# Softcap attention with a two-stage MLP mixer: the second channel product by pairs of batches in Strassen's seven block products

## The chip, the cores and the metric

The kernel runs on one core of one Trainium2 chip. The core has five engines with a queue each: TensorE (PE) for matrix products into PSUM, VectorE (DVE) and ScalarE (ACT) for elementwise work, GpSimd (POOL), and SyncE (SP), which here only issues DMAs. The metric is the device time of one execution in microseconds, lower is better. Before the change it is 588.58 us, the median of 3 runs (588.46 to 589.6).

## The reference

Four batches, 12 heads, 448 positions, 64 wide. The attention output is the input x (4 x 448 x 768) of a mixer with a token product and a channel product:

```python
scores = cap * np.tanh(scale * np.matmul(q, k.transpose(0, 1, 3, 2)) / cap)
attn = np.exp(scores - np.max(scores, axis=-1, keepdims=True))
attn = attn / (np.sum(attn, axis=-1, keepdims=True) + 1e-09)
x = np.matmul(attn, v)                       # heads side by side: (4, 448, 768)
h = np.maximum(x.transpose(0, 2, 1) @ w_tok1, 0.0) @ w_tok2
u = x + h.transpose(0, 2, 1)
h2 = np.maximum(u @ w_ch1, 0.0) @ w_ch2      # 768 -> 1536 -> 768
return (u + h2).astype(np.float32)
```

## The kernel before

The program has an attention part, a token part that is worked in between, and a channel part that is PE work from about 261 us on. Only the channel part changes.

Each batch has u as six chunks of 128 channels by 448 positions. The 1536 hidden channels go in 6 groups (`NG`) of 2 x 128 (`GF`). For each group and batch, `ch1` makes the hidden block (2 x 6 chunks x 3 matmuls = 36), and `ch2` multiplies it by the group's second weights and adds to all six chunks of u (6 x 2 x 3 = 36). Each product takes three matmuls because every operand is split into a high and a low part in a fast fp32 format (`TERMS`: high x high, low x high, high x low). PE does `ch1` of the next batch before `ch2` of the last one.

After `ch1`, ACT applies the ReLU into the high part of `g` (line 859) and DVE makes the low part (862). After each chunk of `ch2`, DVE adds PSUM to u (line 891); in the last group the chunk is stored at once (893). The weights arrive as 64-bit floats and are decoded in thirds of 512 columns, six thirds per group: ACT takes the magnitude (233), DVE clips (239, 240) and puts sign and low bits back (246, 247), ACT makes the high part (256), DVE the low part (260). The second weights of the next group go to a second buffer.

PSUM has eight banks: `ps_a` two tiles of two banks, `ps_b` and `ps_c` two tiles of one bank each.

The order on every engine is written out by a planner in the code (`Plan`): an operation becomes a job with a cost, its dependencies and a slack, and when PE's planned time passes, jobs that are ready are put into their engine's queue, the one with the smallest ready time plus slack first. The queues then run strictly in order. When the token part is done, `order.close()` (in `first_group`) ends the written order and the rest of the program runs in the order in which it was issued.

The last batch of the last group lies in one arm of a branch on the size of `cap`; the other arm is a general version that these inputs don't reach.

## Time and profile before

| | |
|---|---|
| median of 3 runs | 588.58 us |
| the profiled execution | 588.43 us |
| its span, first to last instruction | 586.6 us |
| PE busy | 580.8 us (99%), 3102 matmuls |
| DVE busy | 404.4 us (69%) |
| ACT busy | 255.2 us (44%) |
| POOL busy | 9.2 us (2%) |

Busy shares are means over the span; the parts of the program have different limits, so a stretch is read by itself. The chain of waits is followed back from the last instruction: where it runs on one engine without a break, that engine sets the time there. The mean of a matmul (366 ns) is its latency; matmuls overlap, and the step from one to the next is read from the chain. On DVE too an instruction's duration is longer than the step to the next start.

### The profile page before, as it was taken

What the parts mean: (1) busy time and instruction counts of PE and PEld (TensorE: products, weight loads), DVE (VectorE), ACT (ScalarE), POOL (GpSimd) and SP (SyncE); (2) the same over time, 40 slices, a digit from 0 to 9 for tenths busy, and PEclk for the clock granted to TensorE, in tenths of its full rate; (3) what the DMA queues carried; (4) which work ended last, traced back from release to release, by engine and by line L of the source; (5) the groups of instructions that cost most, each with busy time, mean ns of one, the idle gap of its engine ahead of it and who ended that gap; (6) DMA issues with size and microseconds to landing.
All of it is one profiled execution on the core that took longest, in us unless ns stands there. A gap on an engine that the chain in (4) does not pass through costs nothing.

```text
span 586.6 us, 7996 instructions
## 1 busy us (share of the span) xinstructions
PE 580.8 (99%) x3102; PEld 450.0 (77%) x3102; DVE 404.4 (69%) x681; ACT 255.2 (44%) x330; POOL 9.2 (2%) x23
## 2 busy tenths in 40 slices
PE   8999999999999999999999999999999999999997
PEld 2233455544646899999999999999999999999996
DVE  2999999998999997468886568356834653333334
ACT  6999999899897343241431213021302120000000
POOL 0000100001000000000000000000000000000000
PEclk9999999999999999999999999999999999999999
DMA  7554766857431041002433032103210200000234
GB/s 228 178 155 127 236 194 195 244 168 220 147 120 53 21 136 37 1 1 73 143 108 108 1 108 72 37 0 108 72 37 0 73 1 0 1 0 5 93 112 172
DMA packets 26779, 55.50 MB, mean 95 GB/s; under 512 B 7024, under 2 KB 16752, under 8 KB 26736
## 3 DMA queue, kind: packets, MB, share of 16 engines
q1 hardware_dynamic: 24288, 48.37, 26.6%
q0 software_dynamic: 2160, 6.39, 3.9%
...
q10 hardware_dynamic: 288, 0.18, 0.1%
q14 instruction: 18, 0.15, 0.1%
...
## 4 chain that ended last, share of the span: by engine, by line
PE 90%; ACT 6%; DVE 1%; issue 1%; DMA 1%; DVEq 0%; ACTq 0%
PE ps_g L849 30%; PE ps_o L881 30%; PE ps_pv L438 7%; PE ps_qk L360 6%; PE ps_h L596 5%; PE ps_u L619 5%; ACT e L390 3%; ACT e L398 3%; PE ps_t L568 2%; PE ps_s L489 2%; PE ps_pv L441 1%; PE ps_qk L371 1%; PE ps_qk L365 1%; DMA qkraw<-in_qk 1%; DVE acc L477 0%
## 5 line engine op out<-in xcount | busy, mean ns | idle before, releaser
L881 PE MATMUL ps_o<-g,wc 128*128 128x448 f32 x864 | 181.2, 366 | 0.0
L881 PEld LDWEIGHTS ps_o<-g,wc 128*128 128x128 f32 x864 | 162.0, 188 | 14.4
L849 PE MATMUL ps_g<-uhl,wc 128*128 128x448 f32 x648 | 138.1, 367 | 0.0
L849 PEld LDWEIGHTS ps_g<-uhl,wc 128*128 128x128 f32 x648 | 121.0, 188 | 11.1 <-issue 0.7
L891 DVE TENSOR_TENSOR u<-u,ps_o 128x448 f32<-128x448 f32 (+1 forms) x145 | 87.3, 614 | 43.3 <-PE ps_o L881 42.9
L390 ACT ACTIVATE e<-ps_qk,tsc 128x896 f32<-128x896 f32 x84 | 81.8, 1040 | 9.5 <-PE ps_qk L360 4.2
L398 ACT ACTIVATE e<-e,near 128x896 f32<-128x896 f32 x84 | 85.7, 1082 | 0.1
L859 ACT ACTIVATE g<-ps_g 128x896 fp32r<-128x896 f32 x24 | 22.0, 916 | 134.5 <-PE ps_g L849 134.3
L862 DVE SCALAR_TENSOR_TENSOR g<-ps_g,g 128x896 fp32r<-128x896 f32 x24 | 26.1, 1088 | 72.4 <-ACT g L859 72.4
L438 PE MATMUL ps_pv<-e,vn 128*64 128x448 f32 x288 | 60.5, 549 | 0.9 <-ACT e L398 0.9
L256 ACT ACTIVATE wc<-wz 128x512 fp32r<-128x512 f32 x36 | 22.8, 634 | 84.2 <-DVE wz L247 37.6
L849 PE MATMUL ps_g<-last_u,wc 128*128 128x448 f32 x216 | 45.6, 368 | 0.0
L438 PEld LDWEIGHTS ps_pv<-e,vn 128*64 128x64 f32 x288 | 18.0, 136 | 34.7 <-issue 25.0
L849 PEld LDWEIGHTS ps_g<-last_u,wc 128*128 128x128 f32 x216 | 40.5, 188 | 4.1
L233 ACT ACTIVATE wz<-wraw 128x512 f32<-128x512 f32 x36 | 24.2, 672 | 37.2 <-DVE wc L260 16.9
L260 DVE TENSOR_TENSOR wc<-wz,wc 128x512 fp32r<-128x512 f32 x36 | 24.7, 687 | 20.1 <-ACT wc L256 19.6
L596 PE MATMUL ps_h<-wc,last_u 128*128 128x384 f32 x176 | 33.3, 337 | 0.0
L619 PE MATMUL ps_u<-last_u,wc 128*128 128x448 f32 x144 | 32.9, 372 | 0.0
L596 PEld LDWEIGHTS ps_h<-wc,last_u 128*128 128x128 f32 x176 | 30.8, 188 | 1.8 <-issue 1.3
L619 PEld LDWEIGHTS ps_u<-last_u,wc 128*128 128x128 f32 x144 | 26.4, 188 | 6.0 <-issue 1.8
L477 DVE TENSOR_TENSOR acc<-acc,e 64x448 f32<-64x448 f32 x48 | 29.7, 618 | 1.3
L460 DVE TENSOR_TENSOR acc<-e 128x896 f32<-128x896 f32 x24 | 25.9, 1078 | 6.6 <-ACT e L398 6.5
...
## 6 DMA issues: line engine op xcount, KB each, us to landing
...
vn<-in_v SPq DMA_DIRECT2D x24, 224.0 KB, 3.3
rb<-rs SPq DMA_DIRECT2D x48, 112.0 KB, 3.4
out_t<-u SPq DMA_DIRECT2D x23, 224.0 KB, 1.9
...
```

Of the source, the lines that this page charges most:

```text
L360: nc.tensor.matmul(ps[:, j, :S], two[x][r, ks], two[y][r, :S], start=(n == 0), stop=(n == 2))
L390: nc.scalar.activation(e, ps[:, :, :S], AF.Tanh, scale=tsc)
L398: nc.scalar.activation(e, e, AF.Exp, scale=near)
L438: nc.tensor.matmul(o, vn[x % 3][:, j * NF + c], es[b, p, c][:, j], start=first, stop=last)
L460: nc.vector.tensor_tensor(accs[b, q][0][:, i], es[b, p, 0], es[b, p, 1], op=ALU.add)
L477: nc.vector.tensor_tensor(t, t, es[b, p - i, NF][r, i], op=ALU.add)
L596: nc.tensor.matmul(ps[:, :HALF], w, x, start=(n == 0), stop=(n == len(mm) - 1))
L619: nc.tensor.matmul(ps[:, :S], h1[:, hi, t, cs], w2s[:, wi, t, :], start=(n == 0), stop=(n == 3 * NT - 1))
L849: nc.tensor.matmul(ps[:, i, :S], w[:, wi, cc, fs], uhl[b][:, ui, cc, :], start=(n == 0), stop=(n == 3 * NC - 1))
L862: nc.vector.scalar_tensor_tensor(x[:, 1], ps[:, :, :S], 0.0, x[:, 0], op0=ALU.max, op1=ALU.subtract)
L881: nc.tensor.matmul(ps[:, :S], w[:, wi, i, cs], x[:, gi, i, :], start=(n == 0), stop=(n == 3 * GF - 1))
L891: nc.vector.tensor_tensor(u[b][:, cc, r], u[b][:, cc, r], ps[:, r], op=ALU.add)
```

## The change

From group 1 on the second product is done for two batches together. The hidden blocks of the two batches (h0, h1 of the first, h2, h3 of the second) are seen as a 2 x 2 block matrix, the group's second weights as another (two hidden halves by two output halves of 3 chunks). Strassen's scheme in Winograd's form needs seven block products instead of eight; a block product here is 3 chunks x 3 matmuls. Group 0 stays as it was.

- The ReLU now goes to an fp32 buffer `hid` (line 912 of the changed kernel). POOL forms four differences in place: x = h3 - h2, t1 = x - h0, t2 = h3 - t1, t4 = h1 - t2 (line 927). ACT and DVE split the seven left operands into high and low parts (946, 950), in a ring of six.
- The weights need three block sums and one difference: four DVE operations of 128 columns (279 to 282) per third, and high and low parts of seven blocks instead of four (287, 288 on ACT; 296, 297 on DVE). The seven blocks of a third have one buffer, so the next group's can be written only after this group's last product.
- The products are chained in PSUM. Chain a takes p1, p6, p5, p3, one onto the other, in three banks; chain b takes p7 and p4, then p2 anew, in three more. After each product DVE adds the chain's present sum to the half of u that it belongs to: in chain a the first two chunks with one wide add (1011), else chunk by chunk (1071). So PE may add the next product of a chain to a bank only when DVE has read it.
- A pair's second product is issued after both first products of the next pair; the last two pairs follow each other. In the last group the sums of p4, p5, p2 and p3 are stored as they are added.
- The written order (`order`) now lasts to the end of the program.

```diff
+MC = NC // 2
+NW = 4
+NS = 3
+NO = 6
+PRODUCTS = (
+    ("p1", 0, "h0", "a", 0, 0),
+    ("p7", 1, "x", "b", 1, 1),
+    ("p6", 5, "t2", "a", 1, 0),
+    ("p4", 3, "t4", "b", 1, 0),
+    ("p5", 4, "t1", "a", 1, 1),
+    ("p2", 2, "h1", "b", 0, 0),
+    ("p3", 6, "h3", "a", 0, 1),
+)
...
+            if sums is not None:
+                job("dve", 4 * 190, 4 * 190 + 70, blocks, (*key, 3), ("m2",), room("ws"), slack=slack, key=(*key, 5))
+                return
...
+        def blocks():
+            z = bits(held["z"]).rearrange("p (k c) -> p k c", k=NW)
+            s = held["s"] = late["m2"].tile([P, NS, P], F32, tag="ws", name="ws", bufs=2)
+            held["ws"] = rings["ws"].take(1)
+            add, sub = ALU.add, ALU.subtract
+            nc.vector.tensor_tensor(s[:, 0], z[:, 1], z[:, 3], op=add)
+            nc.vector.tensor_tensor(z[:, 1], z[:, 0], z[:, 1], op=sub)
+            nc.vector.tensor_tensor(s[:, 1], s[:, 0], z[:, 0], op=sub)
+            nc.vector.tensor_tensor(s[:, 2], z[:, 2], s[:, 1], op=sub)
+            job("act", 935, 1040, high, (*key, 5), *after, slack=slack, key=(*key, 4))
+
+        def high():
+            z = bits(held["z"]).rearrange("p (k c) -> p k c", k=NW)
+            nc.scalar.activation(sums[0][:, :NW], z, AF.Copy)
+            nc.scalar.activation(sums[0][:, NW:], held["s"], AF.Copy)
+            j = job(SUB, *((930, 1010) if SUB == "dve" else (2400, 2480)), low, (*key, 4), slack=slack, key=key)
+            held["wz"].read(j)
+            held["ws"].read(j)
+
+        def low():
+            z = bits(held["z"]).rearrange("p (k c) -> p k c", k=NW)
+            e = nc.vector if SUB == "dve" else nc.gpsimd
+            e.tensor_tensor(sums[1][:, :NW], z, sums[0][:, :NW], op=ALU.subtract)
+            e.tensor_tensor(sums[1][:, NW:], held["s"], sums[0][:, NW:], op=ALU.subtract)
...
+    wsum = [wset[i][1][:, :2 * (NW + NS) * P].rearrange("p (x k c) -> p x k c", x=2, k=NW + NS) for i in range(2)]
+    wend = [wset[i][1][:, 2 * (NW + NS) * P:3 * (NW + NS) * P].rearrange("p (k c) -> p k c", k=NW + NS) for i in range(2)]
+    wblock = [(wsum[i][:, 0], wsum[i][:, 1]) for i in range(2)] + [tuple(wend)]
...
+        late["o"] = m1.tile([P, NO, 2, S], F32R, name="ops", bufs=1)
+        late["h"] = m1.tile([P, 5, S], F32, name="hid", bufs=1)
...
+    def relu(g, b, ps, hold):
+        h = late["h"]
+        n, j = (g, b // 2), b % 2
+        old = late.get("last")
+        if j == 0:
+            free = [("s", old, k) for k in ("p4", "p2")] if old else []
+        else:
+            free = [("s", old, k) for k in ("p5", "p3")] if old else []
+
+        def take():
+            nc.scalar.activation(h[:, 2 * j:2 * j + 2], ps[:, :, :S], AF.Relu)
+
+        hold.read(job("act", 891, 960, take, plan.pe + DRAIN, *free, slack=-300.0, key=("r", n, j)))
+        if j == 1:
+            operands(n, old)
+            late["last"] = n
...
+    def operands(n, old):
+        h = late["h"]
+        place = {"h0": 0, "h1": 1, "t1": 2, "h3": 3, "x": 4, "t2": 0, "t4": 0}
+
+        def form(key, out, a, b, *deps):
+            e, cost = (nc.gpsimd, (1170, 1250)) if FORM == "gps" else (nc.vector, (536, 620))
+            job(FORM, *cost, lambda: e.tensor_tensor(h[:, out], h[:, a], h[:, b], op=ALU.subtract),
+                *deps, slack=500.0, key=("f", n, key))
+
+        form("x", 4, 3, 2, ("r", n, 1), *([("s", old, "p7")] if old else []))
+        form("t1", 2, 2, 0, ("f", n, "x"), ("r", n, 0))
+        form("t2", 0, 3, 2, ("f", n, "t1"), ("s", n, "p1"))
+        form("t4", 0, 1, 0, ("f", n, "t2"), ("s", n, "p6"))
+        source = {"h0": ("r", n, 0), "h1": ("f", n, "t4"), "h3": ("f", n, "t2")}
+        before = None
+        for k, _, of, *_ in PRODUCTS:
+            deps = [source.get(of, ("f", n, of)), room("o")] + ([("sh", n, before)] if before else [])
+            split(n, k, h[:, place[of]], deps)
+            before = k
+
+    def split(n, k, src, deps):
+        def high():
+            i = len(rings["o"].holds) % NO
+            t = late["o"][:, i]
+            operand[n, k] = t, rings["o"].take(1)
+            nc.scalar.activation(t[:, 0], src, AF.Copy)
+
+        def low():
+            t = operand[n, k][0]
+            nc.vector.tensor_tensor(t[:, 1], src, t[:, 0], op=ALU.subtract)
+
+        job("act", 468, 568, high, *deps, slack=800.0, key=("sh", n, k))
+        job("dve", 536, 620, low, ("sh", n, k), slack=800.0, key=("s", n, k))
...
+        seen = {"a": 0, "b": 0}
+        for k, a, _, chain, i, j in PRODUCTS:
+            await_key(("s", n, k))
+            x, of = operand[n, k]
+            b = 2 * q + j
+            first = k in ("p1", "p7", "p2")
+            done_now = last and k in ("p4", "p5", "p2", "p3")
+            for mc in range(MC):
+                await_key(("wc2", g, mc))
+                if not first or k == "p2":
+                    await_key(("o", n, chain, mc, seen[chain] - 1))
+                ps = banks[chain][mc]
+                for m, (wi, xi) in enumerate(TERMS):
+                    nc.tensor.matmul(
+                        ps[:, :S], wblock[mc][wi][:, a], x[:, xi], start=first and m == 0, stop=m == 2,
+                        skip_group_check=not first,
+                    )
+                plan.spend(3 * 204)
+                wide = chain == "a" and mc < 2 and not done_now
+                if wide and mc == 0:
+                    continue
+                cc = MC * i + mc
+                if wide:
+                    o = job("dve", 1010, 1092, lambda b=b, cc=cc: add_two_out(b, cc - 1, two), plan.pe + DRAIN, slack=URGENT,
+                            key=("o", n, chain, 0, seen[chain]))
+                    done["o", n, chain, 1, seen[chain]] = o
+                    holds_of["a"][0].read(o)
+                else:
+                    o = job("dve", 530, 612, lambda b=b, cc=cc, ps=ps, d=done_now: add_out(b, cc, ps, d), plan.pe + DRAIN,
+                            slack=URGENT, key=("o", n, chain, mc, seen[chain]))
+                    if chain == "b":
+                        holds_of["b"][mc].read(o)
+                    elif mc == 2:
+                        holds_of["a"][1].read(o)
+                    elif mc == 1:
+                        holds_of["a"][0].read(o)
+                fill()
+            of.read(plan.pe)
+            seen[chain] += 1
+
+    def add_two_out(b, cc, ps):
+        nc.vector.tensor_tensor(u[b][:, cc:cc + 2], u[b][:, cc:cc + 2], ps[:, :, :S], op=ALU.add)
...
-                order.close()
...
+            ch1(w[0], b, g, b // 2)
+            if g == 1 and b == 0:
+                ch2(*pend)
+                done["ch2", 0] = plan.pe
             if g == NG - 1 and b == 0:
                 tc.mark_branch_hint_location("big", hint="LikelyTaken", engines=(engines.PE,))
-            ch2(*pend)
-            if pend[1] == B - 1:
-                done["ch2", pend[4]] = plan.pe
-            pend = (w[1], b, gt, g == NG - 1, g)
+            if b % 2:
+                if before is not None:
+                    ch2_pair(before, False)
+                    if before[1] == 1:
+                        done["ch2", before[0]] = plan.pe
+                before = g, b // 2
...
-        gt = ch1(w[0], B - 1, NG - 1)
-        ch2(*pend)
-        ch2(w[1], B - 1, gt, True, NG - 1)
+        ch1(w[0], B - 1, NG - 1, 1)
+        ch2_pair((NG - 1, 0), True)
+        ch2_pair((NG - 1, 1), True)
```

How this moves instructions. On PE, before: the first product of batch 1 in group 2 and then the second product of batch 0 (`ps_g` is the first product's PSUM tile, `ps_o` the second's, `wc1`, `wc2` the weights, `g` the split hidden block).

```order
L849 MATMUL ps_g_3278<-uhl1_2038,wc1_0_79 128x448 x36
L881 MATMUL ps_o_3333<-g_3213,wc2_0_80 128x448 x6
L881 MATMUL ps_o_3345<-g_3213,wc2_0_80 128x448 x6
L881 MATMUL ps_o_3354<-g_3213,wc2_0_80 128x448 x6
L881 MATMUL ps_o_3363<-g_3213,wc2_0_80 128x448 x6
L881 MATMUL ps_o_3373<-g_3213,wc2_0_80 128x448 x6
```

Now, in group 2: the first product of batch 1, and p1 and p7 of the pair of batches 2 and 3 of group 1 (`ps_o2` is the two-bank tile of chain a, `ops` the ring of split operands).

```order
L1024 MATMUL ps_g_3607<-uhl1_2038,wc1_1_81 128x448 x36
L983 MATMUL ps_o2_3665<-ops_2039,wc2_0_80 128x448 x3
L983 MATMUL ps_o2_3665<-ops_2039,wc2_1_82 128x448 x3
L983 MATMUL ps_o_3666<-ops_2039,wc2_0_80 128x448
L983 MATMUL ps_o_3666<-ops_2039,wc2_1_82 128x448
L983 MATMUL ps_o_3666<-ops_2039,wc2_0_80 128x448
L983 MATMUL ps_o_3667<-ops_2039,wc2_0_80 128x448 x3
L983 MATMUL ps_o_3668<-ops_2039,wc2_1_82 128x448 x3
L983 MATMUL ps_o_3669<-ops_2039,wc2_0_80 128x448
L983 MATMUL ps_o_3669<-ops_2039,wc2_1_82 128x448
L983 MATMUL ps_o_3669<-ops_2039,wc2_0_80 128x448
```

Six matmuls in a row on a bank became three, and the same banks come back after 18 matmuls with the next product of their chain.

On DVE, before: the adds of a second product in group 1, batch 0, between weight decoding (`wz`, `wraw`: the third being decoded).

```order
L891 TENSOR_TENSOR u0_75<-u0_75,ps_o_2921 128x448
L247 SCALAR_TENSOR_TENSOR wz_2979<-wraw_2938,wz_2979 128x512
L891 TENSOR_TENSOR u0_75<-u0_75,ps_o_2928 128x448
L239 TENSOR_SCALAR wz_3182<-wz_3182 128x512
L891 TENSOR_TENSOR u0_75<-u0_75,ps_o_2942 128x448
L260 TENSOR_TENSOR wc2_0_80<-wz_2979,wc2_0_80 128x512
L891 TENSOR_TENSOR u0_75<-u0_75,ps_o_2951 128x448
L240 TENSOR_SCALAR wz_3182<-wz_3182 128x512
L246 SCALAR_TENSOR_TENSOR wz_3182<-wraw_3165,wz_3182 128x512
L891 TENSOR_TENSOR u0_75<-u0_75,ps_o_2961 128x448
L247 SCALAR_TENSOR_TENSOR wz_3182<-wraw_3165,wz_3182 128x512
```

Now, at the start of the pair of batches 2 and 3 of group 1: the last piece of weight decoding in front of it, then the adds of p1, p7, p6 and p4 with two splits (`hid` to `ops`) in between.

```order
L267 SCALAR_TENSOR_TENSOR wz_3652<-wraw_3625,wz_3652 128x512
L1011 TENSOR_TENSOR u2_77<-u2_77,ps_o2_3665 128x896
L1071 TENSOR_TENSOR u2_77<-u2_77,ps_o_3666 128x448
L1071 TENSOR_TENSOR u3_78<-u3_78,ps_o_3667 128x448
L1071 TENSOR_TENSOR u3_78<-u3_78,ps_o_3668 128x448
L950 TENSOR_TENSOR ops_2039<-hid_2040,ops_2039 128x448
L1071 TENSOR_TENSOR u3_78<-u3_78,ps_o_3669 128x448
L1011 TENSOR_TENSOR u2_77<-u2_77,ps_o2_3665 128x896
L950 TENSOR_TENSOR ops_2039<-hid_2040,ops_2039 128x448
L1071 TENSOR_TENSOR u2_77<-u2_77,ps_o_3666 128x448
L1071 TENSOR_TENSOR u2_77<-u2_77,ps_o_3667 128x448
```

Weight decoding was spread between the adds; it now stands between the pairs, and the adds have splits between them.

On DVE at the end, before: the adds to batches 2 and 3 in the last group.

```order
L891 TENSOR_TENSOR u2_77<-u2_77,ps_o_4754 128x448
L891 TENSOR_TENSOR u2_77<-u2_77,ps_o_4763 128x448
L891 TENSOR_TENSOR u3_78<-u3_78,ps_o_4772 128x448
L891 TENSOR_TENSOR u3_78<-u3_78,ps_o_4781 128x448
L891 TENSOR_TENSOR u3_78<-u3_78,ps_o_4790 128x448
L891 TENSOR_TENSOR u3_78<-u3_78,ps_o_4799 128x448
L891 TENSOR_TENSOR u3_78<-u3_78,ps_o_4808 128x448
L891 TENSOR_TENSOR u3_78<-u3_78,ps_o_4817 128x224 x2
```

Now, from one of the last two pairs to the other: the end of the pair of batches 0 and 1, and the start of the pair of batches 2 and 3, with the last splits.

```order
L950 TENSOR_TENSOR ops_2039<-hid_2040,ops_2039 128x448
L1071 TENSOR_TENSOR u1_76<-u1_76,ps_o2_4745 128x448 x2
L1071 TENSOR_TENSOR u1_76<-u1_76,ps_o_4746 128x448
L950 TENSOR_TENSOR ops_2039<-hid_2040,ops_2039 128x448 x2
L1011 TENSOR_TENSOR u2_77<-u2_77,ps_o2_4850 128x896
L1071 TENSOR_TENSOR u2_77<-u2_77,ps_o_4858 128x448
L1071 TENSOR_TENSOR u3_78<-u3_78,ps_o_4859 128x448
L950 TENSOR_TENSOR ops_2039<-hid_2040,ops_2039 128x448
L1071 TENSOR_TENSOR u3_78<-u3_78,ps_o_4860 128x448
L950 TENSOR_TENSOR ops_2039<-hid_2040,ops_2039 128x448
L1071 TENSOR_TENSOR u3_78<-u3_78,ps_o_4861 128x448
```

The splits of the last pair stand before and between its adds.

## Rows read from the trace of the kernel before

**Rows 1.** The page's table of busy time: busy us, share of the span, instructions.

```profile
PE 580.8 (99%) x3102; PEld 450.0 (77%) x3102; DVE 404.4 (69%) x681; ACT 255.2 (44%) x330; POOL 9.2 (2%) x23
```

**Rows 2.** The chain that ended last: start us, us, engine, tile, line, instructions.

```profile
261.38 12.27 PE ps_o L881 x60
...
288.44 7.36 PE ps_o L881 x36
295.80 7.36 PE ps_g L849 x36
...
568.52 14.74 PE ps_o L881 x72
```

**Rows 3.** By stage: us; busy us of PE, PEld, DVE, ACT, POOL; clock, DMA share, GB/s.

```profile
347.40:406.36 58.96, 58.96 (x290) 54.06 (x289) 34.44 (x58) 11.18 (x16) 0.00 (x0) 1.00 0.17 54
```

**Rows 4.** Timeline of VectorE, 262 to 265 us: start us, us, instruction.

```profile
263.35 0.62 DVE L720 TENSOR_TENSOR last_u<-u,last_u 128x448 fp32r<-128x448 f32 x1
263.88 0.61 DVE L891 TENSOR_TENSOR u<-u,ps_o 128x448 f32<-128x448 f32 x1
```

**Rows 5.** Timeline of all engines, 566 to 587 us.

```profile
568.36 14.89 PE L881 MATMUL ps_o<-g,wc 128*128 128x448 f32 x72
...
569.86 0.62 DVE L891 TENSOR_TENSOR u<-u,ps_o 128x448 f32<-128x448 f32 x1 [8.11 <-PE ps_o L881]
570.40 1.08 DVE L862 SCALAR_TENSOR_TENSOR g<-ps_g,g 128x896 fp32r<-128x896 f32 x1
...
571.40 0.61 DVE L891 TENSOR_TENSOR u<-u,ps_o 128x448 f32<-128x448 f32 x1
...
583.28 0.68 DVE L891 TENSOR_TENSOR u<-u,ps_o 128x224 f32<-128x224 f32 x2 [0.61 <-PE ps_o L881]
584.00 0.36 ACTq L893 DMA_DIRECT2D out_t<-u  x1
```

**Rows 6.** Timeline of VectorE, 276 to 281 us.

```profile
276.43 0.43 DVE L239 TENSOR_SCALAR wz<-wz 128x512 f32<-128x512 f32 x1 [1.53 <-ACT wz L233]
...
277.36 0.69 DVE L246 SCALAR_TENSOR_TENSOR wz<-wraw,wz 128x512 int32<-128x512 int32 x1
278.08 0.69 DVE L247 SCALAR_TENSOR_TENSOR wz<-wraw,wz 128x512 int32<-128x512 int32 x1
278.69 0.42 DVE L239 TENSOR_SCALAR wz<-wz 128x512 f32<-128x512 f32 x1
...
279.49 0.69 DVE L260 TENSOR_TENSOR wc<-wz,wc 128x512 fp32r<-128x512 f32 x1
280.09 0.68 DVE L246 SCALAR_TENSOR_TENSOR wz<-wraw,wz 128x512 int32<-128x512 int32 x1
```

**Rows 7.** Groups of instructions by form: busy us, mean ns of one, idle before.

```profile
L256 ACT ACTIVATE wc<-wz 128x512 fp32r<-128x512 f32 x36 | 22.8, 634 | 84.2 <-DVE wz L247 37.6 <-PE ps_g L849 36.0 <-PE ps_o L881 10.1
L859 ACT ACTIVATE g<-ps_g 128x896 fp32r<-128x896 f32 x24 | 22.0, 916 | 134.5 <-PE ps_g L849 134.3
...
L579 DVE TENSOR_TENSOR wc<-ps_t,wc 64x128 fp32r<-64x128 f32 x24 | 7.0, 293 | 0.3
```

**Rows 8.** Groups of instructions by form, GpSimd.

```profile
masks.py:199 POOL TENSOR_SCALAR_AFFINE_SELECT ident<-ident 128x128 f32<-128x128 f32 x1 | 0.3, 287 | 0.1
...
L1074 POOL MEMSET const-float32-1.0<- 128x1 f32 x1 | 0.1, 103 | 0.0
```

**Rows 9.** DMA issues: instructions, KB each, median us to landing.

```profile
out_t<-u SPq DMA_DIRECT2D x23, 224.0 KB, 1.9
...
out_t<-u ACTq DMA_DIRECT2D x1, 112.0 KB, 1.7
```

**Rows 10.** Busy time by stage: the fullest DMA of those read; the stores before the end.

```profile
4.00:8.00 4.00, 3.92 (x12) 1.36 (x12) 0.38 (x3) 1.82 (x2) 0.00 (x0) 1.00 0.95 340
...
580.00:584.00 4.00, 3.25 (x16) 2.63 (x15) 2.15 (x5) 0.00 (x0) 0.00 (x0) 1.00 0.54 206
```

More of the change, by code (lines that the diff above doesn't have):

```diff
@@ L53 @@
 PAIRED = (12, 40)
+SUB = "dve"
+END = 2
+FORM = "gps"
+URGENT = -500.0
 class Job:
@@ L208, in room, with like, decode @@
         return rings[n].room
-    def decode(src, n, hi, lo, early, blank, key, slack, since, after):
+    def like(z, to):
+        return z if len(to.shape) == 2 else z.rearrange("p (f m c) -> p f m c", f=GF, m=2)
+    def decode(src, n, hi, lo, early, blank, key, slack, since, after, sums=None):
         held = {}
@@ L280, in group_weights, with second @@
         t2 = t2.rearrange("p (x f c) -> p x f c", x=2, f=GF)
[L281 to L284 removed]
+        st = kw.pop("stagger", 0.0)
+        slack, since = kw.get("slack", 3000.0), kw.get("since", 0.0) + GF * C * st
+        def second(mc):
+            d = t2.rearrange("p x f (m k c) -> p x f m k c", m=2, k=MC)[:, :, :, :, mc]
+            decode(
+                wc2[g][:, mc * DU:(mc + 1) * DU], DU, d[:, 0], d[:, 1], False, None, ("wc2", g, mc),
+                slack, since + mc * DU * st, after[1], wblock[mc] if combine else None,
+            )
+        return (t1, t2), decode_steps(wc1[g], t1, DU, ("wc1", g), after=after[0], stagger=st, **kw) + [
+            lambda mc=mc: second(mc) for mc in range(MC)
+        ]
     in_att, e_att, x_att = ExitStack(), ExitStack(), ExitStack()
@@ L839, in ch1 @@
+    def add_two_out(b, cc, ps):
+        nc.vector.tensor_tensor(u[b][:, cc:cc + 2], u[b][:, cc:cc + 2], ps[:, :, :S], op=ALU.add)
+    def ch1(w, b, g=0, pair=None):
         await_time(rings["a"].room)
         ps = ps_a.tile([P, 2, 512], F32, tag="a", name="ps_g")
-        hold = rings["a"].take(2)
+        hold = rings["a"].take(2 if pair is None else 1)
         for i in range(GF):
@@ L855, in ch1 @@
             open_m1()
-        x = m1.tile([P, 2, GF, S], F32R, tag="g", name="g")
+        if pair is not None:
+            relu(g, b, ps, hold)
+            return None
+        i = 2 * (late.setdefault("n", 0) % 2)
+        late["n"] += 1
+        x = late["o"][:, i:i + 2]
         def high():
@@ L887, in add_out @@
     def add_out(b, cc, ps, last):
-        end = last and b == B - 1 and cc == NC - 1
+        end = last and b == B - 1 and cc == (END if late.get("last") else NC - 1)
         for i, q in enumerate((nc.sync, nc.scalar) if end else (nc.sync,)):
@@ L918, in open_m2 @@
         split_tile(2, pool)
+        late["m2"] = pool
+        done["m2",] = plan.pe
     def first_group(w):
@@ L945, in tile_softcap_mixer @@
     w = w0
+    before, steps_of = None, {}
     for g in range(NG):
+        later = steps_of[g][-MC:] if g > 1 else []
         if g + 1 < NG:
-            nxt, steps = group_weights(
-                g + 1, ([("tok",)], [("tok",)]) if g == 0 else ((), [("ch2", g - 1)]), slack=60000.0
-            )
-            for step in steps:
-                step()
+            nxt, steps_of[g + 1] = group_weights(
+                g + 1, ([("tok",)] if g == 0 else (), [("ch2", g)]), combine=True, slack=60000.0
+            )
+            later = steps_of[g + 1][:len(steps_of[g + 1]) if g == 0 else -MC] + later
+        for step in later:
+            step()
         if g == 0:
@@ L1000, in general @@
     def general():
+        late.pop("last")
         for step in decode_steps(w1, w1s, DU, ("w1",), False, w1s[:LAST, 1, NK - 1]) + decode_steps(w2, w2s, S, ("w2",)):
@@ L1037, in tile_softcap_mixer @@
         general()
+    order.close()
 def kernel(q, k, v, cap, moe_w_tok1, moe_w_tok2, moe_w_ch1, moe_w_ch2):
```

40 lines of the change are left out of this document (26 added, 14 removed).

## The prediction

> **What bounds the kernel now.** I read the busy table first: TensorE (PE) is busy for 580.8 of 586.6 us, VectorE (DVE) for 404.4, GpSimd (POOL) for 9.2 [rows 1]. A busy PE alone proves little, so I took the chain of waits next: from 261.38 us to 583.26 us it runs over PE alone, in pieces of 7.36 us with 36 matmuls each, channel products one and two in turn [rows 2]. That is 204.5 ns from one matmul to the next (14.74 us / 72), without a gap, at a granted clock of 1.00 (the level of 2.4 GHz) in the group looked at [rows 2, 3]. So in this part every matmul that goes takes 0.2045 us off the end, unless PE comes to wait. The third view is the table by stage: in one group of 58.96 us DVE is busy for 34.44 us, ScalarE (ACT) for 11.18, POOL for none [rows 3]. DVE is the engine to watch: nearly all that the change adds goes there.
>
> **What it removes.** Groups 1 to 5 do the second product with 2 x 63 matmuls instead of 4 x 36 = 144. That is 18 less per group, 90 in all: 90 x 0.2045 = 18.4 us. All of them have the same shape as before and stand on the chain. The order of PE up to the first product of group 1 stays as it is.
>
> **What it adds on DVE.** Start-to-start steps are the price in a queue, not durations. 448 columns step 0.535 us (263.35 to 263.88 [rows 4]); 896 columns out of PSUM 1.00 (570.40 to 571.40 [rows 5]); a 512-column two-input operation 0.60 (279.49 to 280.09), a clip pair 0.93 (276.43 to 277.36), a sign-and-low-bits pair 1.33 (277.36 to 278.69) [rows 6]. No row has 128 columns on 128 partitions; 64x128 lasts 293 ns [rows 7], less the 82 ns by which a 0.617 us add overlaps the next it steps 0.21, and 0.33 where it needs the result before it (dependence costs 0.12: 277.36 to 278.08 is 0.72 against 0.60 [rows 6]).
> - Adds of a pair of batches: four products of chain a at 1.00 + 0.535, three of chain b at 3 x 0.535: 10.95 us (12 x 0.535 = 6.4 before).
> - Splits of operands: 7 x 0.535 = 3.75 us (2 x 1.00 before).
> - A third of the second weights: 0.93 + 1.33 + four block sums 1.08 + low parts of 512 and 384 columns 1.07 = 4.41 us, where it was 0.93 + 1.33 + 0.60 = 2.86. A third of the first weights stays at 2.86.
>
> Per group that is 2 x (10.95 + 3.75) + 3 x 4.41 + 3 x 2.86 = 51.2 us. The same sum for before is 24 x 0.535 + 4 x 1.00 + 6 x 2.86 = 34.0 and the trace has 34.44 [rows 3], so the prices hold. PE's group shrinks to 270 x 0.2045 = 55.2 us. DVE goes from 58% of the group to 93%, and its queue is strictly in order: the question is only where PE waits for it. ACT gets 14 splits of at most 0.63 us and three 384-column high parts more: 11.2 + 8.8 + 1.6 = 21.6 of 55.2, so I cost it at nothing beyond the waits below. SP issues the same loads and stores, in thirds as before; the DMA engines are 0.17 busy in such a group [rows 3], so a load that starts later still lands long before its third is decoded.
>
> **Inside a pair.** Let the 63 matmuls start at 0; three matmuls take 0.613, and an add can start 0.27 after the end of its bank (568.36 + 6 x 0.2045 = 569.59, the add starts at 569.86 [rows 5]). The seven products alternate between chain a and chain b, except that p2 starts b anew, so a bank has one product's time, 1.84 us, and the rest of its own, to be read. The wide add of p1 runs 1.50 to 2.51, then in the queue's order: 2.51 to 4.10 three narrow ones, 4.10 a split, 4.64 the last of p7, 5.17 a split, 5.70 to 6.71 the wide add of p6. Chain a is needed again at 3.68 (p6; read by 2.6) and at 7.36 (p5; read by 6.85): 1.0 and 0.5 us to spare. p5's wide add ends at 10.4 and p3 needs it at 11.04: again 0.5. DVE has 13.1 us of work (10.95 + 4 splits) in PE's 12.9, so a delay in front of the pair is not made up within it: what exceeds 0.5 us becomes a PE wait.
>
> What stands in front: from one pair to the next PE takes 72 + 63 matmuls, 27.6 us; DVE does 14.7 of adds and splits and about 10.9 of weights (the 21.8 of a group, halved), 25.6. It also waits in order: for ACT's high part before a low part (0.63 for 512 columns [rows 7], somewhat over 1.1 with the 384) about once per pair, and for POOL's t4 before one split: t4 starts after the fourth split of the pair at 13.1, ends at 14.2, ACT's part at 14.9, where DVE is free at 14.6, so 0.3 to 0.4. So DVE is through at about 27.2 to 28.5 and the first add comes due at 27.6 + 1.5 = 29.1. The cover is 0.6 to 1.9, plus the 0.5 inside.
>
> **POOL's four subtractions per pair.** No row has POOL at two inputs. Below: its one-input select of 128 columns lasts 287 ns and a one-column memset 103 [rows 8], 1.45 ns a column, so 448 take 0.75. Above: twice that per column, 1.4. I take 1.1, the middle, as both ends count the same columns; 40 of them are off the chain at either end. (The Trainium skill, GPSIMD Engine Reference, section 3.1, states about 2.6 cycles per element at 1.2 GHz for two inputs; that is an estimated 0.97 us and the sum would be the same.) The difference x can't start before the ReLU of the pair's second batch (0.916 [rows 7]), which waits for the split of h3 of the pair before it, at 4.7: x, t1, t2 run from about 5.8 to 9.2.
>
> No row shows whether POOL and DVE delay each other, since POOL never computes beside DVE in this trace. If not, nothing is added. If a split must wait for POOL, it is the one at 8.8, at most until t2 ends: 0.4 on average of the phases, which uses up most of the 0.5 to spare. The Trainium skill, SBUF — State Buffer, "Who interferes with whom", says that a DVE instruction with two SBUF inputs and a GpSimd instruction that reads SBUF exclude each other for a whole instruction; here that would hold for splits and weights, not for adds out of PSUM. No row here shows it; by the page the sum would be near rival 1's, without it at the forecast's lower end.
>
> I put 0.3 us of PE wait on each of the first eight pairs: 2.4 us. Ends: 0, and 1.5 (a 1.33 us weight pair just in front of the first add, which then passes 0.5, and a POOL operation in front of a split).
>
> **The last two pairs** follow each other without a first product between them. Chain a's third bank is read by DVE at about 14.6 of the first one; the second wants it at 12.9 + 1.2 = 14.1: 0.6. DVE then carries two splits and three single adds in place of wide ones: another 0.6 at p6 and p5. Together 1.2 (0 to 3; the upper end also for the branch behind which both lie: in the trace DVE stood idle there, 8.11 us before its add [rows 5], and now finds work at once).
>
> **The end.** Before, one 224 KB sum is stored per six matmuls, 1.23 us, and the last lands 1.7 us after its issue at 584.00 [rows 5, 9]. Now twelve are final within PE's last 6.8 us: 2.75 MB. The stores so far ran at 206 GB/s with the DMA engines 0.54 busy, which scales to 381; the fullest window has 340 at 0.95, so 358 [rows 10]. At 365 twelve take 7.5 us. The first is issued some 5.1 us before PE's end, so the last lands 5.1 less, plus 7.5 plus 1.3 (1.9 to land [rows 9] less 0.6 of transfer): 3.7 after PE's end, against 584.00 + 1.7 - 583.26 = 2.45 before: 1.2 us more. Ends: 0, and 5 if stores can't exceed the 206 GB/s seen.
>
> **Sum** against the profiled execution, 588.43 us (span 586.6 and 1.8 around it; 0.15 under the median 588.58): 588.43 - 18.4 + 2.4 + 1.2 + 1.2 = 574.8 us. That PE stands still for under 2 us at a time leaves me no reason in the rows to expect another clock.
>
> **Rivals.**
> 1. *DVE becomes the bound between pairs.* POOL's operations hold up DVE, 2 x 1.1 us in each of eight periods, and the waits for ACT come out at their upper end: 28.5 + 2.2 = 30.7 against 29.1 + 0.5, 1.1 us of wait; with a block sum or a wait mis-sized by 0.4 it is 1.5. 8 x 1.5 = 12, + 1.2 + 1.2: 584.4. For it: 93% and one queue. Against: most DVE work beside t2 and t4 is adds from PSUM.
> 2. *The stores decide the end*, at 206 GB/s: 2.75 MB in 13.3 us; 574.8 + 3.8 = 578.6. For it: no row has more for stores. Against: the engines were half idle then.
> 3. *The chain of operands decides, and the kernel gets slower.* Place: t2 and t4, which need the split before them, POOL, ACT, DVE in turn, while DVE's queue stands at the next split and everything behind it, adds and weights, stands too. If POOL needs 2.4 us, t2 ends at 12.9, the fourth split comes at 13.7 rather than 12.5, t4 at 16.7, and DVE idles 1.8 more before the next split: 28.5 + 3.0 = 31.5 against 29.6, 1.9 per pair. With rival 1's blocking at that length (another 1.5) it is 3.4 x 8 = 27 us: 588.4 - 18.4 + 27 + 2.4 = 599.4. It turns slower from 2.0 us per pair on ((18.4 - 2.4) / 8). Against: 2.4 is 1.7 times my upper end for POOL.
> 4. *The change doesn't do what it says*: a matmul that adds to a bank read in between steps slower than one in a run of six. At 0.02 us a matmul, 630 x 0.02 = 12.6 us: 574.8 + 12.6 = 587.4, no change that can be told. Against: [rows 2] show one step across bank changes.
>
> **How the numbers follow.** Forecast 0.68, from 570 (no wait, end as before: 588.4 - 18.4) to 578.5; rival 1 0.16; rival 2 0.07; rival 3 0.06; rival 4 0.03. A measurement of this kernel tells 0.2%, 1.2 us, from no change. Forecast, rival 2 and nearly all of rival 1 are faster: 0.91. Same 0.03, from the rest of rival 1 and part of rival 4; slower 0.06. The range goes from 570 up to 583.5, into rival 1; 0.12 lies above it and a little below.
>
> **What would show it.** Right: 774 second-product matmuls instead of 864, still about 204.5 ns apart; 40 POOL subtractions near 1.1 us; DVE over 85% busy from group 1 to 4; PE idle in small pieces, at the wide adds (p5, p3) and in the last pair, under 5 us in sum; the last stores landing close behind each other. Wrong: PE waits of over 1 us at the first product of a pair (then the weights are late, rival 1), splits that wait for ACT behind POOL (rival 3), splits whose duration grows beside POOL (blocking), or a step above 210 ns (rival 4).

## The result and the profile after

The changed kernel takes 572.69 us, the median of 4 runs (572.08 to 572.91), against 588.52 us (587.63 to 589.60) for the kernel before, run beside it: a ratio of 0.9729, 95% interval 0.9711 to 0.9747. The forecast was 574.8. The profiled execution took 572.91 us with a span of 571.1; before it was 588.43 and 586.6, so 15.5 us are to be accounted for.

The page's table of busy time, which answers to [rows 1]:

```profile
PE 561.6 (98%) x3012; PEld 432.1 (76%) x3012; DVE 491.7 (86%) x860; ACT 299.0 (52%) x415; POOL 57.5 (10%) x63
```

There are 90 matmuls less, 87 us more of DVE work and 40 instructions more on POOL. The chain that ended last (start us, us, engine, tile, line, instructions) answers to [rows 2]:

```profile
318.09 13.14 PE ps_o L983 x63
331.23 14.72 PE ps_g L1024 x72
345.95 12.88 PE ps_o L983 x63
...
484.17 12.88 PE ps_o L983 x63
```

From 318 to 511.8 us (497.05 + 14.72, the next piece) it is PE alone; behind that the view follows other engines, although PE's own timeline, below, shows no further wait up to 556 us. A pair's second product takes 12.88 us, 63 x 0.2045: a matmul that adds to a bank read in between steps no slower than one in a run of six. Stages of the program (us; busy us of PE, PEld, DVE, ACT, POOL with counts; granted clock, DMA share, GB/s), the first a whole group as in [rows 3], the others a window of the last stores at full rate and what follows PE's last matmul:

```profile
331.23:386.50 55.27, 55.27 (x272) 50.62 (x271) 51.38 (x94) 19.88 (x33) 9.50 (x8) 1.00 0.19 58
...
563.00:565.00 2.00, 2.00 (x12) 1.83 (x11) 2.00 (x5) 0.00 (x0) 0.00 (x0) 1.00 1.05 402
...
566.56:571.10 4.54, 0.00 (x0) 0.00 (x0) 1.18 (x4) 0.00 (x0) 0.00 (x0) 0.99 0.69 256
```

PE's group is 55.27 us (forecast 55.2), DVE's share of it 51.38 (forecast 51.2). PE's timeline has the places at which it waited, in brackets with the releaser:

```profile
318.09 13.14 PE L983 MATMUL ps_o<-ops,wc 128*128 128x448 f32 x63 [0.49 <-ACT hid L912]
...
539.28 16.97 PE L983 MATMUL ps_o<-ops,wc 128*128 128x448 f32 x81
556.62 3.97 PE L983 MATMUL ps_o<-ops,wc 128*128 128x448 f32 x18 [0.37 <-DVE u L1011]
560.81 5.75 PE L983 MATMUL ps_o<-ops,wc 128*128 128x448 f32 x27 [0.22 <-DVE u L1011]
```

One wait of 0.49 us stands in front of the first pair, none at the next seven, two lie in the last two pairs. A duration in this view holds the last matmul's latency, so a delay is read from start to start: the first pair starts 8.09 us after the 36 matmuls in front of it (310.00 to 318.09), the third one 7.43 (366.03 to 373.46), which makes that wait cost 0.65. PE ends at 566.56; from 539.28 that is 27.28 us for 126 matmuls, whose steps make 25.77 and the last one's end 0.16 more, so 1.35 are lost. The span goes on for 4.54 us after PE, before for 3.34. The sum: -18.4 for the matmuls, +0.65, +1.35, +1.2 for the end, and -0.35 because the channel part starts at 261.02 instead of 261.38 us: -15.55, against -15.5 measured. The -0.35 is not the change's work; the runs below differ by more than that in front of the first pair.

VectorE in front of the first pair (start us, us, instruction), and then GpSimd and ScalarE there:

```profile
304.31 1.35 DVE L308 TENSOR_TENSOR wc<-wz,wc 128x512 fp32r<-128x512 f32 x1 [0.22 <-ACT wc L304]
305.59 1.64 DVE L296 TENSOR_TENSOR wc<-wz,wc 128x512 fp32r<-128x512 f32 x1
307.15 1.51 DVE L297 TENSOR_TENSOR wc<-ws,wc 128x384 fp32r<-128x384 f32 x1
...
311.96 1.53 DVE L267 SCALAR_TENSOR_TENSOR wz<-wraw,wz 128x512 int32<-128x512 int32 x1
...
315.81 0.68 DVE L308 TENSOR_TENSOR wc<-wz,wc 128x512 fp32r<-128x512 f32 x1
316.41 0.62 DVE L950 TENSOR_TENSOR ops<-hid,ops 128x448 fp32r<-128x448 f32 x1
```

```profile
303.85 4.40 POOL L927 TENSOR_TENSOR hid<-hid 128x448 f32<-128x448 f32 x3 [146.71 <-ACT hid L912]
...
317.12 0.92 ACT L912 ACTIVATE hid<-ps_g 128x896 f32<-128x896 f32 x1 [1.17 <-DVE ops L950]
```

The same low part (308) takes 1.35 us beside GpSimd's differences and 0.68 after them. That is the blocking for which the kernel before had no row. Four operations are lengthened here, by 3.4 us together (1.35, 1.64, 1.51 and 1.53 us instead of 0.68, 0.68, 0.55 and 0.69). What PE then waits for is not a weight. Chain a needs a two-bank PSUM tile that the ReLU of an earlier product (912) still has to empty; the ReLU writes into `hid`, and it stands 1.17 us until VectorE has split p2's operand out of there (316.41 to 317.03). That is the way by which VectorE's late queue reaches PE.

Inside a pair the blocking is smaller. In the group from 373.46 us a split lasts 1.03 us instead of 0.61, 8.75 us into the pair, and the wide add that p3 needs stands right behind it:

```profile
382.21 1.03 DVE L950 TENSOR_TENSOR ops<-hid,ops 128x448 fp32r<-128x448 f32 x1
383.17 1.07 DVE L1011 TENSOR_TENSOR u<-u,ps_o 128x896 f32<-128x896 f32 x1
```

### The profile page after: what moved, and what is told of

It reads as the page before. It is cut to its first block, busy times and chain, and to the rows that moved or that the text cites. A ratio compares the mean times of both kernels' runs of the same rounds, so it can differ in the third digit from the quotient of the medians.

```text
span 571.1 us, 8194 instructions
## 1 busy us (share of the span) xinstructions
PE 561.6 (98%) x3012; PEld 432.1 (76%) x3012; DVE 491.7 (86%) x860; ACT 299.0 (52%) x415; POOL 57.5 (10%) x63
## 4 chain that ended last, share of the span: by engine, by line
PE 77%; DVE 8%; ACT 7%; issue 6%; DMA 1%; POOL 1%; POOLq 0%; SPq 0%; DVEq 0%; ACTq 0%
PE ps_g L1024 26%; PE ps_o L983 16%; PE ps_pv L500 7%; PE ps_qk L422 6%; PE ps_h L658 5%; PE ps_u L681 5%; PE ps_o L1061 5%; ACT e L452 3%; ACT e L460 3%; DVE u L1071 2%; PE ps_t L630 2%; PE ps_pv L503 1%; PE ps_s L551 1%; DVE ops L950 1%; PE ps_qk L433 1%
## 5 line engine op out<-in xcount | busy, mean ns | idle before, releaser
L983 PE MATMUL ps_o<-ops,wc 128*128 128x448 f32 x630 | 131.1, 367 | 1.1 <-DVE u L1011 0.6
L983 PEld LDWEIGHTS ps_o<-ops,wc 128*128 128x128 f32 x630 | 117.6, 188 | 13.3 <-issue 1.6
L1071 DVE TENSOR_TENSOR u<-u,ps_o 128x448 f32<-128x448 f32 (+1 forms) x163 | 92.0, 607 | 10.7 <-PE ps_o L1061 10.6
L946 ACT ACTIVATE ops<-hid 128x448 fp32r<-128x448 f32 x70 | 38.8, 574 | 115.5 <-POOL hid L927 70.3
L927 POOL TENSOR_TENSOR hid<-hid 128x448 f32<-128x448 f32 x40 | 48.2, 1204 | 348.4 <-ACT hid L912 306.2
L1011 DVE TENSOR_TENSOR u<-u,ps_o 128x896 f32<-128x896 f32 x36 | 38.8, 1078 | 17.4 <-PE ps_o L983 17.4
L950 DVE TENSOR_TENSOR ops<-hid,ops 128x448 fp32r<-128x448 f32 x70 | 45.8, 671 | 1.7 <-ACT ops L946 1.7
L912 ACT ACTIVATE hid<-ps_g 128x896 f32<-128x896 f32 x20 | 18.4, 921 | 24.5 <-PE ps_g L1024 19.8
```

What stands on the lines that cost most here:

```text
L927: job(FORM, *cost, lambda: e.tensor_tensor(h[:, out], h[:, a], h[:, b], op=ALU.subtract), *deps, slack=500.0, key=("f", n, key))
L946: nc.scalar.activation(t[:, 0], src, AF.Copy)
L950: nc.vector.tensor_tensor(t[:, 1], src, t[:, 0], op=ALU.subtract)
L983: nc.tensor.matmul(ps[:, :S], wblock[mc][wi][:, a], x[:, xi], start=first and m == 0, stop=m == 2, skip_group_check=not first,)
L1011: nc.vector.tensor_tensor(u[b][:, cc:cc + 2], u[b][:, cc:cc + 2], ps[:, :, :S], op=ALU.add)
L1071: nc.vector.tensor_tensor(u[b][:, cc, r], u[b][:, cc, r], ps[:, r], op=ALU.add)
```

## The experiments

All times are medians, beside the kernel before in the same runs. PE is ready for the first pair between 317.3 and 319.6 us in the traces read here, and by up to 2 us apart even where the edits touch only the end; so where an edit is worth about 1 us I compare stretches of the traces from there on.

**1. Blocking or mere load.** POOL keeps as busy but reads nothing; the differences are left out.

```diff
-            job(FORM, *cost, lambda: e.tensor_tensor(h[:, out], h[:, a], h[:, b], op=ALU.subtract),
+            job(FORM, *cost, lambda: [e.memset(h[:, out], 0.0) for _ in range(3)],
```

> The changed kernel, with each difference on GpSimd replaced by three memsets of the same 448 columns (the differences are left out, so the products work on zeros): GpSimd is busy for about as long but reads nothing from SBUF. Theory A (a VectorE operation with two SBUF inputs and a GpSimd operation that reads SBUF exclude each other): VectorE's splits go back from 671 to about 617 ns on average and no 512-column operation lasts over 0.8 us; the wait of 0.5 us before the first pair goes, the rest stays: 572.0 to 572.5. Theory B (GpSimd slows VectorE by being busy, whatever it reads): durations as in the changed kernel, 572.7.

572.38 us, ratio 0.9727 (0.9712 to 0.9742). Groups of the changed kernel (busy us, mean ns of one | idle before), and then of this one:

```profile
L927 POOL TENSOR_TENSOR hid<-hid 128x448 f32<-128x448 f32 x40 | 48.2, 1204 | 348.4 <-ACT hid L912 306.2 <-DVE ops L950 40.6
L950 DVE TENSOR_TENSOR ops<-hid,ops 128x448 fp32r<-128x448 f32 x70 | 45.8, 671 | 1.7 <-ACT ops L946 1.7
```

```profile
L927 POOL MEMSET hid<- 128x448 f32 x117 | 54.3, 474 | 301.0 <-ACT hid L912 254.1 <-DVE ops L950 42.2 <-issue 0.3
L950 DVE TENSOR_TENSOR ops<-hid,ops 128x448 fp32r<-128x448 f32 x70 | 42.2, 618 | 3.5 <-ACT ops L946 3.5
```

With POOL busy for longer, the splits are back at 618 ns, DVE's busy time over the span falls from 491.7 to 485.2 us, and the 0.49 us wait before the first pair is gone. So reads by POOL hold DVE up by 6.5 us in all, 1.0 us per full group (51.4 to 50.4). Nearly all of it lies under cover, that is, PE does not wait for it: the two kernels' times are 0.3 us apart, within their intervals. The Trainium skill, SBUF — State Buffer, "Who interferes with whom", says just this: a DVE instruction with two SBUF inputs contends with a GpSimd instruction that reads SBUF, not with one that only writes; both traces agree.

**2. The differences on VectorE**: `FORM = "dve"`.

> The changed kernel, with the four differences of a pair on VectorE instead of GpSimd (40 x 0.535 = 21.4 us more on VectorE, nothing on GpSimd). Theory A (VectorE's work inside a pair decides: 13.1 us in TensorE's 12.9 with 0.5 us to spare): three of the four differences fall into the pair, 1.6 us more, so about 1.1 us of TensorE wait per pair, 11 us in all: 584, with waits at the wide adds. Theory B (only the sum of a group decides): the group has 51.4 us of VectorE work in the trace of the changed kernel, less about 1.2 us that two-input operations lost beside GpSimd, plus 4.3: 54.5 of 55.3, so nearly no wait: 572 to 575.

584.68 us, ratio 0.9934 (0.9918 to 0.9950): theory A's number, but not at its place. PE's timeline, here at the third pair:

```profile
373.50 1.39 PE L983 MATMUL ps_o<-ops,wc 128*128 128x448 f32 x6
376.07 0.47 PE L983 MATMUL ps_o<-ops,wc 128*128 128x448 f32 x1 [1.18 <-ACT wc L287]
377.54 13.28 PE L983 MATMUL ps_o<-ops,wc 128*128 128x448 f32 x56 [0.99 <-DVE wc L296]
```

PE waits for the last third of the second weights, at the first product of a group's first pair; it does so in three groups and never at the second pair. This is rival 1's mechanism, DVE as the bound between pairs, here by four differences of 0.535 us, 2.1 us of DVE work per pair, instead of blocking. The time is near rival 1's 584.4, but not by its sum of 1.5 in each of eight pairs: the groups last 59.6, 58.0 and 58.0 us instead of 55.3, and the last two pairs take 1.7 us more (28.94 instead of 27.28). In the first of the groups the clock adds to it; the stage just behind the waits:

```profile
378.00:382.00 4.00, 4.00 (x15) 3.56 (x15) 2.81 (x5) 2.07 (x3) 0.00 (x0) 0.66 0.02 4
```

**3. POOL's differences at twice the length.**

```diff
+        def twice(e, o, x, y):
+            e.tensor_tensor(o, x, y, op=ALU.subtract)
+            e.tensor_tensor(o, o, nc.const_aps.tensor(0.0, [P, S]), op=ALU.add)
...
+            job(FORM, *cost, lambda: twice(e, h[:, out], h[:, a], h[:, b]),
```

> The changed kernel, with a second GpSimd operation behind each difference (it adds a constant zero to it), so that each difference takes GpSimd about 2.4 us instead of 1.2; the queues' order is the same. Rival 3 of the prediction gave this case its price: 1.9 us of TensorE wait per pair without blocking and 3.4 with it, so 8 x 1.9 = 15 to 27 us: 588 to 600. The rival theory: the trace of the changed kernel has no TensorE wait at all from the second pair to the eighth, so there is cover that the prediction did not see; if it is over 3 us per pair this costs under 5 us: below 578. In both, two-input VectorE operations beside GpSimd get longer in more places.

580.54 us, ratio 0.9863 (0.9847 to 0.9878): 7.9 us above the changed kernel and between the two theories. The wait is not spread over the pairs:

```profile
321.57 14.66 PE L987 MATMUL ps_o<-ops,wc 128*128 128x448 f32 x63 [3.31 <-ACT hid L912]
```

```profile
321.57:325.00 3.43, 3.43 (x9) 3.08 (x10) 0.79 (x1) 0.04 (x1) 0.00 (x0) 0.51 0.04 16
```

The first pair waits 3.31 us, and after it the granted clock is 0.51 for 3.4 us, the lower of its two levels, 1.2 GHz: the 63 matmuls take 1.5 us more. Of the next seven pairs four lose nothing and three, each the second of its group, 0.6 to 1.3 us; the last two lose 1.7. Rival 3 had 1.9 in every pair for POOL at 2.4 us, so its chain of operands is better covered than it assumed.

**4. and 5. Where the cover lies.** The low parts of a third of the second weights are computed again, one of them (small) or both (large).

```diff
             e.tensor_tensor(sums[1][:, NW:], held["s"], sums[0][:, NW:], op=ALU.subtract)
+            e.tensor_tensor(sums[1][:, :NW], z, sums[0][:, :NW], op=ALU.subtract)   # large only
+            e.tensor_tensor(sums[1][:, NW:], held["s"], sums[0][:, NW:], op=ALU.subtract)
```

> The 384-column low part of each third of the second weights is computed twice (0.47 us each, 1.4 us of VectorE per group). Theory A (as the prediction counted, cover of 0.6 to 1.9 us in front of each pair and 0.5 inside, the weights spread evenly over both pairs): 0.7 us per pair is hidden, 572.7. Theory B (all three thirds of the second weights are decoded in front of the first pair of a group, where VectorE has no idle time; the last third is ready at 373.42 and wanted at 374.69, so 1.27 us are to spare): 1.4 - 1.3 = 0.1 per group in four groups, and up to 1.4 once before the first pair, which already waits: 573 to 574.5.

> Both low parts of each third of the second weights are computed twice (1.07 us each, 3.2 us of VectorE per group, 54.6 of 55.3). Theory A (even cover): 1.6 us per pair against 1.1 to 2.4 to spare, at most 0.5 x 8 = 4 us: 572.7 to 576.5, with the waits at the wide adds inside the pairs. Theory B (the place decides): 3.2 - 1.3 - 0.2 = 1.7 us of wait in each of four groups, all of it at the first product of the group's first pair for the weights, and up to 3.2 once at the very first pair: 579.5 to 583, while VectorE still idles about 1 us or more per group in front of the second pair.

Small: 575.96 us, 0.9783 (0.9768 to 0.9798). Large: 583.83 us, 0.9912 (0.9894 to 0.9930). Both are theory B, though 1.5 and 0.8 us above its ranges. PE's timeline, small and then large:

```profile
320.37 13.14 PE L984 MATMUL ps_o<-ops,wc 128*128 128x448 f32 x63 [2.11 <-ACT hid L913]
...
442.85 2.08 PE L984 MATMUL ps_o<-ops,wc 128*128 128x448 f32 x9 [0.25 <-DVE u L1012]
```

```profile
321.81 15.65 PE L985 MATMUL ps_o<-ops,wc 128*128 128x448 f32 x63 [3.62 <-ACT hid L914]
...
382.48 11.90 PE L985 MATMUL ps_o<-ops,wc 128*128 128x448 f32 x56 [1.19 <-DVE wc L298]
```

With 1.4 us more a group's first pair starts on time and PE waits at the wide add in front of p3, the place the prediction named for a delay that is not made up inside the pair. The groups last 55.5, 55.8 and 55.8 us instead of 55.3, so 0.9 to 1.2 of the 1.4 us are covered. With 3.2 us more the weights themselves are late. The first pair of all has no cover (1.6 us more of wait for 1.4 us of work); there the clock is what I had left out of the large one. Its stages, PE's wait and the matmuls after it:

```profile
318.20:321.81 3.61, 0.00 (x0) 0.00 (x0) 3.15 (x6) 2.16 (x4) 0.00 (x0) 0.83 0.88 252
321.81:325.00 3.19, 3.19 (x9) 2.84 (x10) 0.54 (x1) 0.00 (x0) 0.00 (x0) 0.50 0.11 44
```

After the 2.11 us of the small one the clock stays at 1.00; after 3.62 us it is 0.50, and 63 matmuls take 15.65 us instead of 13.14. The length of the wait alone does not decide it. In the large one the clock falls a second time, to 0.68 from 497 to 500 us, behind waits of 0.17 and 1.33 us:

```profile
495.07 0.47 PE L985 MATMUL ps_o<-ops,wc 128*128 128x448 f32 x1 [0.17 <-ACT wc L287]
496.87 13.26 PE L985 MATMUL ps_o<-ops,wc 128*128 128x448 f32 x56 [1.33 <-DVE wc L298]
```

The same 56 matmuls took 11.90 us behind the wait of 1.19 us above. In experiment 2 the clock falls behind 1.18 and 0.99 us and not behind 1.01 and 0.99. The four runs of the large one go from 582.73 to 586.12 us in the order of their mean granted clock (0.997 to 0.990). What makes it fall is open.

**6. Another order of the products**: p1, p2, p6, p7, p5, p4, p3.

```diff
     ("p1", 0, "h0", "a", 0, 0),
+    ("p2", 2, "h1", "b", 0, 0),
+    ("p6", 5, "t2", "a", 1, 0),
     ("p7", 1, "x", "b", 1, 1),
...
```

> The changed kernel with the seven products in the order p1, p2, p6, p7, p5, p4, p3 (chain b takes p2 first and then p7 and p4), everything else the same. In the last pair three of the twelve stores then come at the second product instead of within the last four. Theory A (the 1.2 us longer end is the queue of stores on the DMA engines): the end after TensorE's last matmul goes from 4.5 us back to 3.4 to 3.7, 571.7 or a little less. Theory B (the longer end is something else, such as VectorE being behind with its adds): it stays at 4.5, 572.7.

577.32 us, ratio 0.9817 (0.9803 to 0.9830): both theories missed the time. The end that they were about is 4.2 us behind PE (574.6 - 570.4), nearer to theory B. VectorE's timeline in a pair, and PE's:

```profile
381.67 1.56 DVE L950 TENSOR_TENSOR ops<-hid,ops 128x448 fp32r<-128x448 f32 x1
383.15 0.61 DVE L1071 TENSOR_TENSOR u<-u,ps_o 128x448 f32<-128x448 f32 x1
383.68 1.07 DVE L1011 TENSOR_TENSOR u<-u,ps_o 128x896 f32<-128x896 f32 x1
```

```profile
384.90 2.08 PE L983 MATMUL ps_o<-ops,wc 128*128 128x448 f32 x9 [0.21 <-DVE u L1011]
...
559.08 11.28 PE L983 MATMUL ps_o<-ops,wc 128*128 128x448 f32 x54 [2.06 <-DVE u L1071]
```

The split now stands one narrow add earlier in DVE's queue, and it ends at the same time as before (383.23 and 383.24 us), when POOL has ended its run of three: it is held for 0.95 instead of 0.42. The narrow add that was in front of it is now behind it, the wide add comes 0.5 us later (383.68 against 383.17), and the last product waits. One place in DVE's queue was the difference between a covered delay and 0.6 to 1.0 us per group; the last pair adds a wait of 2.06. The wait before the first pair is gone here (7.44 us from start to start), as p2's operand is split earlier.

**7. The bank of the last pair.**

```diff
-        for tag in ("b", "b", "c", "c"):
+        for tag in (("c", "c", "b", "b") if last and q == 1 else ("b", "b", "c", "c")):
```

> Only the last pair's banks change places: its chain a takes for its third bank the one that the pair before it leaves earlier. Theory A (the 0.37 us wait of TensorE at 556.6 us is for that bank alone): the wait goes, 0.3 to 0.6 us less than the changed kernel, 572.1 to 572.4. Theory B (VectorE's queue is full from 548 us to the end, so a wait that is taken away comes back at the next add): 572.7 within 0.15, TensorE's waits in the last two pairs still 0.6 us in sum.

572.34 us, ratio 0.9723 (0.9710 to 0.9737). PE's last two pairs take 27.26 us (27.28 before this edit), and the waits are 0.62 and 0.22 us. The other bank does take away 0.24 us, inside the first 81 matmuls (16.73 us instead of 16.97), and the next wait, for a wide add, is 0.25 longer. Theory B: a wait that is taken away there comes back at the next add.

**8. and 9. The stores.** Of the last pair's 12 sums six are stored or, in the second, one (11 are left out, where the expectation says 23).

```diff
-            if last:
+            if last and (b < B - 2 or cc % 2 == 0 or end):    # the second: (b < B - 2 or end)
```

> In the last pair of batches only every second 224 KB sum of the output is stored (and the very last one), so the other stores of that pair are left out. Theory A (the stores of twelve sums at some 400 GB/s set the end, as the term of 1.2 us has it): the span ends 2.3 to 3 us after TensorE instead of 4.5: 570.4 to 571.3. Theory B (the last add and the time for one store to land set the end): 4.2 to 4.5 us after TensorE as now, 572.3 to 572.7.

> In the last pair of batches only the very last 224 KB sum is stored (the other 23 stores of that pair are left out). With half the stores left out the span ended 4.23 us after TensorE instead of 4.54. Theory A (what is left is the last add, 1.18 us behind TensorE, and the landing of one store, 2.6 us in the kernel before): 3.8 us after TensorE, 571.9 to 572.3. Theory B (the landing always takes what it takes with half the stores, 3.0 us): 4.2 us, 572.6.

572.91 us, 0.9735 (0.9717 to 0.9753), and 573.46 us, 0.9739 (0.9719 to 0.9759). The span ends 4.23 us (571.2 - 566.97) and 4.10 us (572.5 - 568.40) after PE. Theory B both times: transfers are worth 0.44 of the 4.54 us, not more.

**10. to 12. Two places mended**: the first pair's differences on VectorE; three low parts of the last pair on GpSimd; both.

```diff
+            on = "dve" if n == (1, 0) else FORM
...
+        late_split = n == (NG - 1, 1) and k in ("p5", "p2", "p3")
+        job(*(("gps", 1170, 1250) if late_split else ("dve", 536, 620)), low, ("sh", n, k), slack=800.0, key=("s", n, k))
```

> The four differences of the first pair of batches (the pair at 318 us) are computed by VectorE, the other 36 by GpSimd as in the changed kernel. Theory A (the wait of 0.49 us before that pair is there because operations with two SBUF inputs took twice their time beside GpSimd: 1.35 to 1.64 us against 0.69): the four run 0.62 us each on VectorE, less than the 2.5 us that five lengthened operations gain, the wait goes, 0.3 to 0.5 us less: 572.2 to 572.4. Theory B (VectorE had too much to do there in any case): the wait stays or grows by the 2.1 us of added work, 572.7 to 574.5.

> In the last pair of batches the low parts of the operands of p5, p2 and p3 are computed by GpSimd, 1.6 us less for VectorE's queue between 549 and 559 us. Theory A (the two waits of TensorE in the last two pairs, 0.37 and 0.22 us, and the adds that end 1.18 us behind TensorE, all come from VectorE's full queue): the second wait goes, the last add ends 0.75 us behind, 0.4 to 0.9 us less: 571.8 to 572.3. Theory B (GpSimd's reads hold up the splits and the operands come late): TensorE waits for operands at p5 or p2, 573 to 574.

> Both of the last two edits in one: the first pair's differences on VectorE, and three low parts of the last pair on GpSimd. If both hold, the gains add up: 571.3 to 571.9. If only one does, 572.2; if VectorE's load is what counts in both places, 572.7 or more.

572.48 us, 0.9732 (0.9714 to 0.9750); 572.61 us, 0.9724 (0.9704 to 0.9743); both together 570.55 us, 0.9692 (0.9675 to 0.9709). Singly the medians cannot be told from the changed kernel, though each takes its own wait away in its trace (7.44 us in front of the first pair; 26.20 us for the last two pairs). Together they are 2.1 us below it, and the intervals just don't meet. PE's timeline of both together, and VectorE's last adds:

```profile
311.36 7.60 PE L1027 MATMUL ps_g<-last_u,wc 128*128 128x448 f32 x36
318.80 13.04 PE L986 MATMUL ps_o<-ops,wc 128*128 128x448 f32 x63
...
539.79 26.23 PE L986 MATMUL ps_o<-ops,wc 128*128 128x448 f32 x126
...
565.45 1.75 DVE L1074 TENSOR_TENSOR u<-u,ps_o 128x448 f32<-128x448 f32 x4 [0.40 <-PE ps_o L986]
```

No wait is left from the first pair on. By place: 7.44 us from the last first product to the first pair where it was 8.09 (310.00 to 318.09), 26.23 for the last two pairs instead of 27.28, 4.28 after PE instead of 4.54: 2.0 us. The lag of the last add behind PE stayed at 1.2 us although DVE had idled 0.4 us just before, so a full queue does not explain that one. The lines do: the last three sums need four adds (the last sum in halves), 1.75 us, and the first of them starts at 565.45, when PE has ended the second sum (566.02 - 0.61), though the first sum was done 0.6 us before that. The first two lie in chain a's one two-bank tile; that the tile ties them is likely, but no run tests it.

## Why the prediction was right, and what was off

- *The matmuls* (-18.4): right. 630 matmuls at 0.2045 us (12.88 us per pair), which ends rival 4.
- *DVE's work* (51.2 per group) and *POOL at 1.1 us*: right, 51.38 and 1.20 (1.15 undisturbed, up to 1.53 beside DVE). The 51.38 hold 1.0 of blocking, so the instructions themselves were over-priced by about 0.8.
- *0.3 us in each of eight pairs* (+2.4): the mis-sized term; it measured 0.65 in all, at the first pair only. Its parts were right one by one: the split 8.8 us into the pair was held for 0.42 (0.4 forecast), and 0.5 was to spare; the cover in front of a group's first pair is 0.9 to 1.2 (0.6 to 1.9 forecast; the 28.5 behind the 0.6 is more than its own items give, 25.6 + 1.2 + 0.4 = 27.2). A delay under its slack costs nothing, and I charged a mean over cases that include late ones. That no first pair of groups 2 to 4 waits inside is partly luck: the wide add in front of p3 ends at 384.24 us and p3 is due at 384.50, and where PE did wait it started 0.15 after such an add (experiment 6), so 0.1 us was left. What I didn't see is that the first pair of all has the full blocking and no cover, with four lengthened weight operations in its queue, and that this reaches PE through the ReLU and a PSUM tile.
- *That the weights lie evenly over both pairs*: wrong, without effect on the time. The second weights' thirds stand in front of the group's first pair, and there, not at the wide adds, PE waits once DVE gets 3.2 us more per group in front of it, or 2.1 per pair (experiments 5 and 2). Rival 1 was thus real and close: 3.2 us of DVE work per group, and a clock that falls after some of the waits, cost 11 us.
- *The last two pairs* (+1.2): 1.35, right in size. Half of it was put on the bank, which is worth nothing by itself (experiment 7); DVE's queue was the cause (11).
- *The end* (+1.2): 1.20, right in size for the wrong reason. The stores run at 402 GB/s, faster than the 365 assumed, and their transfers are 0.44 of it; 0.48 is the last add, 1.18 us behind PE's end instead of 0.70, because the first of the last three sums is added late (12), and some 0.3 is unexplained. The sum came out since my 2.45 for before left out 0.9 us that both kernels spend between the landing and the end of the span. Rival 2 falls with it; its 578.6 was also added up too low, as 13.3 us of stores instead of 7.5 are 5.8 more by the same sum, 580.6.
- *The range's lower end*, 570, was the case of no wait and the old end; the version without waits, still with the longer end, measures 570.55.
